# Reordering the start of a fused Fourier-filter and SiLU-MLP kernel: t2 loads between the filters and the weights, six stage-1 result tiles, four inverse tiles, weight roundings behind the groups, three vector pieces moved

## The chip, the cores and the metric

One core of one Trainium2 chip. The metric is the device time of one execution in microseconds (us); every time below is a median of several executions. Profiles are of one execution each, so a profile's span can differ from the median by a few us. In the lines of the profile PE is TensorE (matmuls), PEld its weight loads, DVE VectorE, ACT ScalarE and POOL GpSimd; SPq and ACTq are the queues on which the sync engine and ScalarE issue DMAs. L198 is line 198 of the kernel of that run, "x4" four instructions merged into one line, and a bracket tells how long the engine was idle before and what ended it.

## The reference, cut to what matters

```python
# x: (8, 3008, 256) float32; filters: (1505, 256); weights float64
X = np.fft.rfft(x, axis=1)
y = np.fft.irfft(X * (filt_r + 1j * filt_i)[None], n=3008, axis=1)     # global filter
h = y.reshape(8 * 3008, 256) @ w_in                                     # 256 -> 2048
g = h * (1 / (1 + np.exp(-h)))                                          # silu
return g @ w_out                                                        # 2048 -> 256
```

## The kernel before

The kernel does the Fourier part as matmuls in four stages per batch: sums and stage 1 (results `t1`, stored to DRAM as `d1`), six groups of forward transform, filter product and inverse transform (load `t2`, multiply, add, inverse, result tiles `q`, stored as `d2`), and stage 3 (load `t4`, results `y`). The MLP runs in 384 "hidden steps" and fills TensorE. Batches 1 to 7 do their Fourier part beside the steps of the batch before; batch 0 has nothing to hide behind. Its Fourier part and the conversion of the float64 weights ("roundings", 16 of them, on DVE, ACT and GpSimd) are the ramp. The parts concerned:

```python
def load_filters():                       # 16 DMAs, each to 16 partitions, 12 rows of 1 KB
    for j in range(4):
        for half in range(2):
            for k, filt in enumerate((filt_r, filt_i)):
                nc.sync.dma_start(out=f_t[k][p0:p0 + 16]..., in_=...)
...
def stage1(u):
    t1 = tpool.tile(..., tag="t")         # two buffers, shared with t2
    ...                                   # four matmuls, two copies out of PSUM
    nc.gpsimd.dma_start(out=d1..., in_=t1...)     # twice
...
weights(0); load_filters()                # the ramp's order
# sums and stage1, u = 0..7
load_t2(0); load_t2(1); e_t; weights(1); weights(2); wi_t
rounded(0); rounded(1)
for g in range(6):
    forward(g)                            # its end loads t2 of g + 2
    multiply(g, 0); multiply(g, 1)        # DVE
    add(g, 0); add(g, 1)                  # GpSimd in batch 0
    if g > 0: inverse(g - 1)              # its copies, then four stores issued by ACT
    if g % 2 == 0: weights(3 + g // 2)
    rounded(2 + g)
inverse(5); load_t4(0); rounded(8); rounded(9)
# stage3(0..3); then the steps, with rounded(10..15) in steps 0 to 5
```

```python
def plan(b, part):                        # batches 1 to 7; at = first step of batch b
    put(at - 49, 0, load_x, 0); put(at - 49, 0, load_x, 1)
    for u in range(8):
        put(at + u - 48, 5, sums, u); put(at + u - 47, 3, stage1, u)
    ...
    for g in range(NG):                   # every third step from at - 37
        put(at + 3 * g - 37, 3, forward, g) ...
```

## Time and profile before

| | before |
|---|---|
| median (4 executions) | 2746.07 us (2745.39 to 2747.09) |
| TensorE busy | 2630.5 of 2745.5 us |
| first t2 load issued | 63.66 us |
| multiplies of groups 0 to 5 start | 71.0, 80.3, 89.1, 98.4, 107.1, 116.3 |
| t4 load issued | 130.84 |
| first matmul of step 0 | 146.43 |
| step 7 starts | 206.3 |

How to read it: TensorE is busy for 96% of the span, so I looked for time to win where it idles: nearly all before 200 us, the rest in small holes. The start of a step is read off one instruction which each step has once (ACT's first copy of `px`); the difference of such starts between two kernels shows in which step time was won. For step 0 this line reads, before and in the changed kernel:

```profile
147.66 0.37 ACT L447 COPY abc<-px 128x256 f32<-128x256 f32 x1 [1.33 <-PE px L439]
```
```profile
127.86 0.37 ACT L459 COPY abc<-px 128x256 f32<-128x256 f32 x1 [1.33 <-PE px L451]
```

### The profile page before, as it was taken

What the parts mean: (1) busy time and instruction counts of PE and PEld (TensorE: products, weight loads), DVE (VectorE), ACT (ScalarE), POOL (GpSimd) and SP (SyncE); (2) the same over time, 40 slices, a digit from 0 to 9 for tenths busy, and PEclk for the clock granted to TensorE, in tenths of its full rate; (3) what the DMA queues carried; (4) which work ended last, traced back from release to release, by engine and by line L of the source; (5) the groups of instructions that cost most, each with busy time, mean ns of one, the idle gap of its engine ahead of it and who ended that gap; (6) DMA issues with size and microseconds to landing.
All of it is one profiled execution on the core that took longest, in us unless ns stands there. A gap on an engine that the chain in (4) does not pass through costs nothing.

```text
span 2745.5 us, 45764 instructions
## 1 busy us (share of the span) xinstructions
PE 2630.5 (96%) x17664; PEld 2198.8 (80%) x17664; DVE 1652.4 (60%) x3492; ACT 1098.9 (40%) x2994; POOL 506.0 (18%) x738
## 2 busy tenths in 40 slices
PE   2489999999999999999999999999999999999998
PEld 0368889788887888878887888878888788898987
DVE  3676655666556665666656665566655666555555
ACT  1244344433444334443444434444344433444443
POOL 2541210211111111112111121022111211110100
PEclk9789999999999999999999999999999999999999
DMA  9643221331214221332113312133121421110000
GB/s 176 192 125 79 49 46 32 88 79 40 46 37 105 65 50 23 71 85 68 35 33 82 81 47 44 35 82 85 39 47 31 107 65 43 32 27 20 9 16 15
DMA packets 187929, 166.94 MB, mean 61 GB/s; under 512 B 122176, under 2 KB 155584, under 8 KB 187456
## 3 DMA queue, kind: packets, MB, share of 16 engines
q1 hardware_dynamic: 165912, 111.89, 18.0%
q0 software_dynamic: 16256, 47.20, 6.8%
q10 hardware_dynamic: 5544, 4.93, 0.8%
q8 instruction: 138, 2.26, 0.3%
q14 instruction: 79, 0.65, 0.1%
HBM read 88.96 MB, written 74.97 MB: 60 GB/s over the span
## 4 chain that ended last, share of the span: by engine, by line
PE 90%; DVE 4%; DMA 2%; ACT 1%; issue 1%; ACTq 0%; SPq 0%; POOL 0%; DVEq 0%; POOLq 0%
PE acc L495 40%; PE px L439 24%; PE pyz L439 17%; PE pc L330 3%; PE pd L358 3%; PE pa L277 2%; PE pb L300 2%; DMA d<-t 1%; DVE g L410 1%; DVE u L265 1%; DMA x<-in_x_dram 1%; ACTq L338 0%; DVE z L321 0%; DMA raw<-in_moe_w_out_dram 0%; DVE z L320 0%
## 5 line engine op out<-in xcount | busy, mean ns | idle before, releaser
L495 PE MATMUL acc<-g,w_t 128*128 128x256 f32 (+1 forms) x5376 | 1512.5, 375 | 0.4 <-DVE g L410 0.4
L495 PEld LDWEIGHTS acc<-g,w_t 128*128 128x128 f32 x5376 | 1021.9, 190 | 115.6 <-DVE g L410 0.8
L410 DVE TENSOR_TENSOR g<-pyz,abc 128x256 f32<-128x256 f32 (+1 forms) x1152 | 478.2, 415 | 569.3 <-ACT abc L460 323.0
L410 DVE TENSOR_TENSOR g<-g 128x256 f32<-128x256 f32 (+3 forms) x1152 | 611.8, 531 | 196.6 <-ACT g L443 183.4
L439 PE MATMUL px<-ty,w_t 128*128 128x256 f32 (+1 forms) x2304 | 695.4, 383 | 3.5 <-ACT abc L454 2.9
L443 ACT ACTIVATE g<-g 128x256 f32<-128x256 f32 (+1 forms) x1152 | 472.8, 410 | 244.8 <-DVE g L410 244.8
L439 PEld LDWEIGHTS px<-ty,w_t 128*128 128x128 f32 x2304 | 420.5, 190 | 128.5 <-issue 71.0
L439 PE MATMUL pyz<-y,w_t 128*128 128x256 f32 (+1 forms) x1536 | 456.3, 379 | 10.9 <-DVE g L410 10.9
L410 POOL TENSOR_TENSOR s<-s 128x256 f32<-128x256 f32 (+1 forms) x329 | 266.4, 827 | 1022.2 <-DVE s L513 999.0
L439 PEld LDWEIGHTS pyz<-y,w_t 128*128 128x128 f32 x1536 | 282.0, 189 | 58.8 <-DVE g L410 20.1
L454 ACT COPY abc<-px 128x256 f32<-128x256 f32 (+1 forms) x384 | 141.2, 368 | 373.3 <-PE px L439 373.3
L443 ACT ACTIVATE g<-px 128x256 f32<-128x256 f32 (+1 forms) x384 | 145.8, 380 | 302.1 <-PE px L439 302.1
L460 ACT COPY abc<-px 128x256 f32<-128x256 f32 (+1 forms) x384 | 142.9, 372 | 285.2 <-PE px L439 284.9
L338 POOL DMA_DIRECT2D d<-q x168 | 99.3, 598 | 713.5 <-DVE q L208 705.6
L439 PE MATMUL px<-y,w_t 128*128 128x256 f32 (+1 forms) x768 | 226.2, 376 | 1.0 <-ACT y L210 1.0
L439 PE MATMUL pyz<-ty,w_t 128*128 128x256 f32 (+1 forms) x768 | 226.7, 377 | 0.0
L439 PEld LDWEIGHTS pyz<-ty,w_t 128*128 128x128 f32 x768 | 145.2, 190 | 19.0 <-DVE g L410 2.9
L439 PEld LDWEIGHTS px<-y,w_t 128*128 128x128 f32 x768 | 144.3, 190 | 19.6 <-ACT y L210 1.1
L447 ACT COPY abc<-px 128x256 f32<-128x256 f32 (+1 forms) x384 | 134.1, 349 | 1.3 <-PE px L439 1.3
L282 POOL DMA_DIRECT2D d<-t x128 | 65.6, 516 | 332.1 <-ACT abc L460 283.7
L330 PE MATMUL pc<-z,e_t 64*128 64x256 f32 x768 | 106.0, 413 | 16.0 <-POOL z L320 13.4
L208 DVE COPY y<-pd 128x376 f32<-128x376 f32 x64 | 51.7, 808 | 100.7 <-PE pd L358 100.7
(49 smaller groups left out, 1306.9 us busy)
## 6 DMA issues: line engine op xcount, KB each, us to landing
d<-t POOLq DMA_DIRECT2D x128, 192.0 KB, 3.0
t<-d SPq DMA_DIRECT2D x96, 256.0 KB, 3.9
t<-d SPq DMA_DIRECT2D x128, 192.0 KB, 3.9
d<-q POOLq DMA_DIRECT2D x168, 128.0 KB, 2.6
out_dram<-o SPq DMA_DIRECT2D x636, 32.0 KB, 1.8
x<-in_x_dram SPq DMA_DIRECT2D x120, 128.0 KB, 3.0
x<-in_x_dram SPq DMA_DIRECT2D x120, 60.0 KB, 2.9
raw<-in_moe_w_in_dram SPq DMA_DIRECT2D x16, 256.0 KB, 4.8
```

The lines of the kernel that those rows point to most:

```text
L277: nc.tensor.matmul(out=ps[h][64 * par:64 * par + 64], lhsT=wf_t[rows, par], rhs=ut[rows, par], start=True, stop=True)
L282: nc.gpsimd.dma_start(out=d1[par].rearrange("s p n c -> (s p) n c")[:, 4 * u:4 * u + 4, :], in_=t1[64 * par:64 * par + 2 * NS].rearrange(" ...
L330: nc.tensor.matmul(out=ps[i][:, k, :], lhsT=e_t[rows, g, k, ri, :], rhs=zs[k][rows, ri, :], start=(ri == 0), stop=(ri == 1))
L338: queue.dma_start(out=d2[a0:a0 + 2, :, :].rearrange("s n c -> n s c"), in_=qt[64 * p:64 * p + 64, :, :])
L358: nc.tensor.matmul(out=ps[h][c0:c0 + 64, cb, i, :], lhsT=t4s[g][rows, i, 128 * cb + c0:128 * cb + c0 + 64], rhs=wi_t[rows, :], start=True, ...
L410: eng.tensor_tensor(out=out, in0=in0, in1=in1, op=op)
L439: nc.tensor.matmul(out=out, lhsT=w_t[:, c, 0, jp], rhs=rhs, start=start, stop=True, skip_group_check=True)
L443: nc.scalar.activation(out=g[:, k, 0:n], in_=g[:, k, 0:n] if src is None else src, func=AFT.Silu)
L447: nc.scalar.copy(out=sums[:, 0, 0:n], in_=xo)
L454: nc.scalar.copy(out=sums[:, 1, 0:n], in_=xo)
L460: nc.scalar.copy(out=sums[:, 2, 0:n], in_=xo)
L495: nc.tensor.matmul(out=acc[pair][i][:, h, 0:n], lhsT=w_t[:, c, 1, jp], rhs=g[:, k, 0:n], start=(jp == 0 and h == 0), stop=last, skip_group ...
```

## The change

Intent: give stage 1 so many result tiles that hardly a copy waits for a store, let the first t2 loads pass two thirds of the filters and all later weights, take the weight roundings out of the groups' path, and move three vector pieces of the steady part away from busy places. The core of the diff:

```diff
-    def load_filters():
+    def load_filters(first, last):
...
+            if b > 0 or u < 2 or u > 5:
+                t1 = tpool.tile(..., tag="t")
+            elif u < 4:
+                t1 = typool.tile(..., tag="ty")
+            else:
+                t1 = us["t1"][:, u - 4]          # a tile of the g pool
...
-            eng = nc.vector if b > 0 else nc.gpsimd
+            eng = nc.vector if b > 0 or (g == NG - 1 and k == 0) else nc.gpsimd
...
+                if b > 0 or i == 0:
+                    qt = qpool.tile(..., tag="q")
+                else:
+                    qt = opool.tile(..., tag="o")
...
-                    queue = nc.gpsimd if b > 0 else nc.scalar
+                    queue = nc.gpsimd if b > 0 or (g == NG - 1 and i == 0) else nc.scalar
...
-        put(at - 49, 0, part["load_x"], 0)                 # and 1
+        put(at - 51, 0, part["load_x"], 0)
-            put(at + u - 48, 5, part["sums"], u)
+            put(at + u - (48 if u else 49), 5, part["sums"], u)
-        for g in range(NG):                                # steps 3 g - 37
+        for g, step in enumerate((-37, -34, -31, -28, -25, -21)):
+            late = 4 if g == 4 else 0                      # group 4's adds half a step later
...
-    load_filters()
+    load_filters(0, 4)
...
-    weights(1)
-    weights(2)
         part["forward"](g)
+        if g == 0:
+            load_filters(4, 2 * NG)
+        if g < 3:
+            weights(1 + g)
         ...                                                # multiplies, adds
+        if 2 <= g < NG - 1:
+            rounded(g)
         if g > 0:
             part["inverse"](g - 1)
-        rounded(2 + g)
     part["inverse"](NG - 1)
+    weights(4)
     part["load_t4"](0)
-    rounded(8)
-    rounded(9)
+    for j in range(5, 9):
+        rounded(j)                                         # weights(5) after j = 5
...                                                        # rounded(9..15) in steps 0 to 5, two of them in step 5
-    stores: ((28, 5), (29, 1))
+    stores: ((30, 1), (30, 5))
```

More of the change, by code (lines that the diff above doesn't have):

```diff
@@ L198, in load_filters @@
                     nc.sync.dma_start(
-                        out=f_t[k][p0:p0 + 16].rearrange("p g k c -> p (g k) c"),
-                        in_=bass.AP(tensor=filt.tensor, offset=filt.offset + off * C,
-                                    ap=[[94 * C, 16], [t * C, 2 * NG], [1, C]]))
+                        out=f_t[k][p0:p0 + 16].rearrange("p g k c -> p (g k) c")[:, first:last],
+                        in_=bass.AP(tensor=filt.tensor, offset=filt.offset + (off + t * first) * C,
+                                    ap=[[94 * C, 16], [t * C, last - first], [1, C]]))
     flip = [0]
@@ L236, in load_x @@
                 queue = (nc.sync, nc.scalar)[u % 2]
+                if u == 0:
+                    us["t1"] = gpool.tile([128, 2, 2, 2, C], FP32, name="t1_g", tag="g")
                 if u in (0, 2):
@@ L271, in stage1 @@
             ut = us.pop(u)
-            t1 = tpool.tile([128, 2, 2, C], FP32, name=f"t1_{b}_{u}", tag="t")
+            if b > 0 or u < 2 or u > 5:
+                t1 = tpool.tile([128, 2, 2, C], FP32, name=f"t1_{b}_{u}", tag="t")
+            elif u < 4:
+                t1 = typool.tile([128, 2, 2, C], FP32, name=f"t1_{b}_{u}", tag="ty")
+            else:
+                t1 = us["t1"][:, u - 4]
             ps = [bank(b, f"pa_{b}_{u}_{h}") for h in range(2)]
@@ L332, in inverse @@
             for i in range(2):
-                qt = qpool.tile([128, 2, C], FP32, name=f"q_{b}_{g}_{i}", tag="q")
+                if b > 0 or i == 0:
+                    qt = qpool.tile([128, 2, C], FP32, name=f"q_{b}_{g}_{i}", tag="q")
+                else:
+                    qt = opool.tile([128, 2, C], FP32, name=f"q_{b}_{g}_{i}", tag="o")
                 evac(qt, ps[i])
@@ L379, in plan @@
         at = STEPS * b
-        put(at - 49, 0, part["load_x"], 0)
-        put(at - 49, 0, part["load_x"], 1)
+        put(at - 51, 0, part["load_x"], 0)
+        put(at - 51, 0, part["load_x"], 1)
         for u in range(8):
-            put(at + u - 48, 5, part["sums"], u)
+            put(at + u - (48 if u else 49), 5, part["sums"], u)
             put(at + u - 47, 3, part["stage1"], u)
@@ L386, in plan @@
         put(at - 39, 0, part["load_t2"], 1)
-        for g in range(NG):
-            put(at + 3 * g - 37, 3, part["forward"], g)
-            put(at + 3 * g - 37, 5, part["multiply"], g, 0)
-            put(at + 3 * g - 36, 1, part["multiply"], g, 1)
-            put(at + 3 * g - 36, 5, part["add"], g, 0)
-            put(at + 3 * g - 35, 1, part["add"], g, 1)
-            put(at + 3 * g - 35, 3, part["inverse"], g)
+        for g, step in enumerate((-37, -34, -31, -28, -25, -21)):
+            late = 4 if g == 4 else 0
+            put(at + step, 3, part["forward"], g)
+            put(at + step, 5, part["multiply"], g, 0)
+            put(at + step + 1, 1, part["multiply"], g, 1)
+            put(at + step + 1, 5 + late, part["add"], g, 0)
+            put(at + step + 2, 1 + late, part["add"], g, 1)
+            put(at + step + (3 if late else 2), 3, part["inverse"], g)
         put(at - 18, 5, part["load_t4"], 0)
@@ L641 @@
     nc.sync.dma_start(out=e_t, in_=e_dram.ap())
-    weights(1)
-    weights(2)
-    nc.sync.dma_start(out=wi_t, in_=wi_dram.ap())
     rounded(0)
@@ L648 @@
         part["forward"](g)
+        if g == 0:
+            load_filters(4, 2 * NG)
+            nc.sync.dma_start(out=wi_t, in_=wi_dram.ap())
+        if g < 3:
+            weights(1 + g)
         for k in range(2):
@@ L652 @@
             part["add"](g, k)
+        if 2 <= g < NG - 1:
+            rounded(g)
         if g > 0:
             part["inverse"](g - 1)
-        if g % 2 == 0:
-            weights(3 + g // 2)
-        rounded(2 + g)
     part["inverse"](NG - 1)
+    weights(4)
     part["load_t4"](0)
-    rounded(8)
-    rounded(9)
+    for j in range(5, 9):
+        rounded(j)
+        if j == 5:
+            weights(5)
     for g in range(4):
@@ L667 @@
         plan(b, spectral(b))
-    for k in range(6):
-        put(k, 1, rounded, 10 + k)
-        if k in (1, 3):
-            put(k, 1, weights, 6 + k // 2)
+    for j in range(9, NJ):
+        put(*((j - 9, 1) if j < NJ - 1 else (5, 5)), rounded, j)
+        if j in (11, 13):
+            put(j - 9, 1, weights, j // 2 + 1)
     per = len(PAIRS) * 2
-    stores = (((10, 1), (10, 5)), ((19, 5), (20, 1)), ((28, 5), (29, 1)), ((34, 1), (34, 5)),
+    stores = (((10, 1), (10, 5)), ((19, 5), (20, 1)), ((30, 1), (30, 5)), ((34, 1), (34, 5)),
               ((42, 1), (42, 5)), ((50, 1), (51, 1)))
```

## The prediction

> **What bounds the kernel now.** I read the slices of the page first, then busy time by stretch, then the waits of the first 260 us, the sync engine's queue in that stretch, and last the few places where TensorE still idles later. The page, 40 slices of 68.6 us, and its span line:
>
> ```profile
> span 2745.5 us, 45764 instructions
> PE   2489999999999999999999999999999999999998
> PEclk9789999999999999999999999999999999999999
> ```
>
> TensorE is full from the fourth slice to the end: 2630.5 of 2745.5 us busy. Idle is 115 us in all, so a change that adds and removes no matmul (this one doesn't) can win at most 115/2746 = 4.2%, and only in the ramp (three slices) or in small holes later. By stretch (columns: stretch, length, busy us of PE, weight load, DVE, ACT, POOL, then granted clock, DMA share, GB/s):
>
> ```profile
> 60.00:80.00 20.00, 8.88 (x80) 4.59 (x80) 9.86 (x18) 3.70 (x6) 9.91 (x15) 1.00 0.89 282
> 80.00:100.00 20.00, 10.98 (x128) 6.66 (x128) 14.52 (x24) 3.66 (x6) 13.86 (x19) 0.91 0.95 254
> 191.00:200.00 9.00, 7.95 (x40) 5.68 (x39) 8.09 (x15) 4.03 (x10) 4.56 (x6) 1.00 0.22 70
> 206.80:213.00 6.20, 6.20 (x33) 4.51 (x32) 3.94 (x9) 2.32 (x6) 1.00 (x2) 1.00 0.15 34
> ```
>
> The ramp is bound by DMA and by chains, not by one engine. From 146 to 200 us the first six hidden steps run with DVE about 90% busy (8.09 of 9.00): step starts, read off the first ACT copy of each, are 147.7, 155.6, 164.6, 173.2, 181.8, 190.5 and 199.1, so 8.6 us a step against 7.26 once the roundings are over. The ramp's waits (engine, line waited for, us, times, longest), and the sync engine's issues (start, length):
>
> ```profile
> ACT t L210 <- DMA d<-t: 38.2, 6, 16.4
> DVE t L208 <- DMA d<-t: 34.7, 5, 14.5
> PE pb L300 <- DMA t<-d: 28.7, 6, 20.0
> ```
> ```profile
> 20.64 0.51 SPq L198 DMA_DIRECT2D filt<-in_filt_r_dram  x1
> 44.34 0.32 SPq L198 DMA_DIRECT2D filt<-in_filt_i_dram  x1
> 63.66 2.71 SPq L289 DMA_DIRECT2D t<-d  x4
> 130.84 13.76 SPq L344 DMA_DIRECT2D t<-d  x10
> ```
>
> Stage 1 has data by 17.5 us, but its result tiles (two buffers) wait for their stores, and the stores share the DMA engines with 3.1 MB of filters until 58 us. So the first t2 load starts at 63.66. Then six groups run at 9.0 us each (first multiplies at 80.3, 89.1, 98.4, 107.1, 116.3); the load of t4 is issued at 130.84 and step 0 begins at 146.4.
>
> The steady holes: all windows from 300 to 2527 us together show 9.35 us without TensorE, about 1.5 us a batch, in two places. One, on DVE at the batch boundary (start, length):
>
> ```profile
> 486.36 0.65 DVE L513 COPY s<-acc 128x480 f32<-128x480 f32 x1
> 486.93 1.78 DVE L265 TENSOR_TENSOR u<-x 111x512 f32<-111x512 f32 x2
> 488.63 0.40 DVE L515 COPY s<-acc 128x240 f32<-128x240 f32 x1
> 488.95 0.41 DVE L410 TENSOR_TENSOR g<-pyz,abc 128x256 f32<-128x256 f32 x1
> ```
>
> The sums of the next batch stand between two drain copies and hold back the g that TensorE's next matmul waits for (0.97 us). The other is at 332 to 335 us: the adds of group 4 (0.42 and 0.92) stand between the same copies, 0.57 us.
>
> **What the Trainium skill says.** (1) "SBUF — State Buffer", section "Door 1: The DMA port swizzle": partitions 0 to 15 reach 4 of 16 ports, measured there at 104 GB/s. A filter DMA writes 16 partitions; the trace agrees: 192 KB every 1.85 us is 106 GB/s, while weights and tables to 128 partitions moved at 370 to 400. (2) "DMA: Bandwidth & Descriptors", "Queues, rings and completion order": each DMA engine consumes the descriptors of one ring in order. The trace agrees: the t2 load of group 2, issued at 77.45 behind two pairs of weights, let its matmul start only at 84.32. (3) "SBUF — State Buffer", "SBUF: two separate sides": VectorE and GpSimd share a port pair which one instruction holds to its end. The trace agrees: a rounding's DVE piece of 0.42 takes 0.94 beside a GpSimd piece. (4) "TensorE: Matmul & The Clock Gate", "What's actually happening": idle windows halve the clock; here 0.59 to 0.70 was granted at 100 to 160 us. The changed ramp has gaps too, so I credit nothing for the clock.
>
> **The change, part by part.**
>
> Stage 1 (six result tiles, a third of the filters ahead of the t2 loads). Results 0 to 5 no longer wait for a buffer; 6 and 7 wait for the stores of 0 and 1, which land at 25 to 26 us as before. All evacuations are done by about 27 us, all stores issued by 28 (eight pairs at 1 us of POOL). Bytes from 17.5 us on: d table and first weights 1.84 MB at some 400 GB/s, 4.6 us; filters 1.05 MB (was 3.15) at 106, 9.9 us; t1 stores 3.1 MB at 250 to 300 GB/s (they ended alone at about that rate at 62 us), 11 us. Sum 25.5 us if nothing overlaps: 43 us. Check on before: from 26.9 to 57.9, 2.75 MB of filters (26 us) plus 1.5 MB of stores (5.5) make 31.5; it took 31.0. So the t2 load starts at about 43 instead of 63.7: -20.7. Roundings 0 and 1 fit in 36 to 42.
>
> Groups. Group 0 shifts with it: forward at 46.5, multiplies 50 to 52.5; group 1 follows at 52.6 to 55, for the rounding between them is gone. Then the remaining filters come in the sync queue after t2 of group 2: 2.1 MB at 106 GB/s is 20 us, starting at about 54, with 0.5 MB of d2 stores beside (2 us): the multiplies of group 2 start at 76 (were at 89.1). So the roundings taken out of the groups gain little there; the filters take their place. Behind them, in order, come weights 1, t2 of group 3, weights 2, t2 of 4, weights 3, t2 of 5. With one group's d2 stores each is 2.1 MB at 275 GB/s (mean of 75 to 100 us), 7.6 us: t2 lands at 82, 89.5 and 97. DVE needs 2.4 (multiplies) + 3.2 (rounding) + 0.6 (copy) = 6.2 a group, POOL 2.8 + 1.4 + sometimes 2.9 = 7.1, both below 7.6. Group 5: multiplies 97.5 to 100, its adds halved by the move of one to DVE, inverse matmuls to 107, copies and stores landed at 111 (before: 14.5 us from multiply to t4, now about 13.5). The load of t4 starts 20 us earlier.
>
> Stage 3. Before it took 15.6 us from t4's issue to step 0. Now four roundings (5 to 8) at 3.3 us, 13 us of DVE, lie between the last inverse and the evacuations: from 107 to 120, while stage 3 can have its matmuls from 115 on; and 1 MB of weights stands before the second t4 load. I add 2.5 us: step 0 at 111 + 18 = 129, -17.5.
>
> Steps 0 to 5. Before, six roundings lie in them; now seven, the last two both in step 5, where DVE is full: +2.7. The batch-1 sums leave step 0 (1.5 us of DVE) but stand before its first combine and wait for x, whose loads are issued only after the last t4 load (144.6 before; 3.3 us to landing): +0.8. Sum +3.5.
>
> Steady state. Sums one step earlier: 6 x 0.97 = 5.8. Group 4's adds later: 7 x 0.57 = 4.0. I take 8.5 of these 9.8; the new places (step 47, steps 25 to 30) have DVE below 65%.
>
> Sum: -17.5 + 3.5 - 8.5 = -22.5; 2745.9 - 22.5 = 2723.
>
> **Rivals.** (a) The filters don't hold the groups: they move beside other traffic, group 2 starts at about 65, and groups run at DVE's and POOL's 6 to 7 us.[...] Against: DMA share was 0.9 to 1.0 while filters ran at 104 to 140 GB/s. Then t4 would load at some 98, the four roundings would bind stage 3, and the time would be about 2712. (b) The stores of t1 don't gain: their tiles are free, but the same engines serve them, and a queue with more stores outstanding is no faster; the t2 load would start at about 52, filters and all behind it by 9 later: 2732. (c) DVE takes the gain back: roundings before stage 3 and in step 5, each 4.3 instead of 3.3 because POOL's products stand beside them, and the moved adds meet other pieces: 2730 to 2735.
>
> **Range and chances.** The ramp sum is uncertain by about 8 either way, the steady part by 3. I predict 2723, with 2710 to 2736. A gain over 2% would need a time under 2691, that is 55 of the 115 us; a loss over 2% would need a broken order of buffers.
>
> **What would show it.** The t2 load at 43 (40 to 47); multiplies of group 2 waiting for the filters' DMA, starting near 76; t4 loading near 111; step 0 near 129 and step 5 over 11 us long; no wait of TensorE over 0.3 us for g at the batch boundary. It is wrong if group 2 starts before 68 or the t2 load after 50, or if the steady windows still lack 1.5 us a batch.

## The result, and the profile after

The changed kernel takes 2717.35 us (2717.07 to 2718.15, 4 executions) against 2746.07: ratio 0.9896, interval 0.9878 to 0.9913. Ratios are the mean time of one kernel's runs over that of the other's of the same rounds, so they are not quite the ratio of the medians quoted. It is 28.7 us faster, 1%, and lies inside the predicted range (2710 to 2736), 5.6 below the predicted 2723.

The page's span and slices of the changed kernel:

```profile
span 2716.4 us, 45798 instructions
PE   4589999999999999999999999999999999999998
PEclk9699999999999999999999999999999999999999
```

The first slice is fuller than before (4 against 2). TensorE's busy sum is 2626.7 us, so it still idles for 89.7 us (before 115.0). The sync engine's issues (start, length):

```profile
38.83 2.75 SPq L296 DMA_DIRECT2D t<-d  x4
47.02 0.60 SPq L198 DMA_DIRECT2D filt<-in_filt_r_dram  x1
63.74 0.32 SPq L198 DMA_DIRECT2D filt<-in_filt_i_dram  x1
108.57 0.80 SPq L354 DMA_DIRECT2D t<-d  x2
```

The first t2 load goes out at 38.8 (was 63.7). The second part of the filters takes the queue from 47.0 to 63.7 and the t4 load comes at 108.6 (was 130.8). What the filters do to the groups stands on DVE, in order of time (last column: idle before, and what ended it):

```profile
54.28 0.69 DVE L208 COPY q<-pc 128x512 f32<-128x512 f32 x1
71.55 0.69 DVE L319 TENSOR_TENSOR z<-pb,filt 128x512 f32<-128x512 f32 x1 [16.58 <-DMA filt<-in_filt_r_dram]
80.67 0.69 DVE L319 TENSOR_TENSOR z<-pb,filt 128x512 f32<-128x512 f32 x1 [1.96 <-PE pb L307]
```

Group 2's multiplies wait 16.6 us for the filters and start at 71.6, 17.5 us earlier than before, though group 0's started 25.3 earlier (45.7). The late part by stretch, columns as in the prediction:

```profile
300.00:2500.00 2200.00, 2199.64 (x14852) 1859.25 (x14851) 1340.89 (x2875) 913.96 (x2515) 373.31 (x553) 1.00 0.24 56
```

0.36 us of 2200 without TensorE: the two holes of each batch are gone. At the batch boundary DVE now reads

```profile
463.53 1.28 DVE L267 TENSOR_TENSOR u<-x 111x512 f32<-111x512 f32 x2
469.44 0.65 DVE L525 COPY s<-acc 128x480 f32<-128x480 f32 x1
470.27 0.41 DVE L527 COPY s<-acc 128x240 f32<-128x240 f32 x1 [0.17 <-PE acc L507]
470.70 0.42 DVE L422 TENSOR_TENSOR g<-pyz,abc 128x256 f32<-128x256 f32 x1
```

with the sums 6 us ahead of the drain copies instead of between them. The account by step starts of both profiles (differences of the starts, us):

| stretch | before | changed | difference |
|---|---|---|---|
| to the start of step 0 | 147.66 | 127.86 | -19.80 |
| step 0 | 7.92 | 8.41 | +0.49 |
| steps 1 to 4 | 34.87 | 34.48 | -0.39 |
| step 5 | 8.62 | 11.41 | +2.79 |
| step 6 | 7.27 | 8.44 | +1.17 |
| step 7 to the end | 2539.16 | 2525.80 | -13.36 |
| span | 2745.5 | 2716.4 | -29.1 |

### The profile page after: what moved, and what is told of

Read it like the earlier page. It is cut to its first block, busy times and chain, and to the rows that moved or that the text cites. A ratio compares the mean times of both kernels' runs of the same rounds, so it can differ in the third digit from the quotient of the medians. Undisturbed runs are those within 1.5% of the kernel's fastest.

```text
span 2716.4 us, 45798 instructions
## 1 busy us (share of the span) xinstructions
PE 2626.7 (97%) x17664; PEld 2203.4 (81%) x17664; DVE 1654.5 (61%) x3494; ACT 1099.1 (40%) x2994; POOL 505.1 (19%) x738
## 4 chain that ended last, share of the span: by engine, by line
PE 93%; DMA 3%; DVE 2%; issue 1%; ACT 1%; SPq 0%; POOL 0%; ACTq 0%; DVEq 0%
PE acc L507 41%; PE px L451 25%; PE pyz L451 18%; PE pc L337 3%; PE pd L368 2%; PE pa L284 2%; PE pb L307 2%; DMA x<-in_x_dram 1%; DVE g L422 0%; DMA filt<-in_filt_i_dram 0%; DMA raw<-in_moe_w_out_dram 0%; DVE u L267 0%; DMA e_t<-e_tbl 0%; DMA d<-q 0%; DMA t<-d 0%
## 5 line engine op out<-in xcount | busy, mean ns | idle before, releaser
L451 PEld LDWEIGHTS px<-y,w_t 128*128 128x128 f32 x768 | 144.6, 190 | 22.5 <-issue 3.0
```

The source lines that it names most:

```text
L451: nc.tensor.matmul(out=out, lhsT=w_t[:, c, 0, jp], rhs=rhs, start=start, stop=True, skip_group_check=True)
```

## The experiments

All runs gave a correct result but one. Because chips and calls differ by about 1 us, each is compared with the kernel before of the same call; "against the changed kernel" compares these differences (the changed kernel: -28.7). Medians of four executions each. Executions of one kernel spread over 1 to 7 us, so differences under about 3 us between two versions are not settled by time alone, and I say where the profile decides.

### e_steady: the steady moves alone

```diff
  (the kernel before, with only plan() and the third store pair of the change)
```

> The kernel before with only the moves in the plan of batches 1 to 7 (x loads two steps and the first sums one step earlier, group 4's adds half a step later, group 5 one step later, the third store pair moved). Theory (the moves themselves close the two holes per batch): 13 us less than before, about 2733, and no wait of TensorE for g over 0.3 us after step 7. Rival (the holes went because the new ramp shifts the batches against their transfers): no gain, about 2746.

2739.48 against 2745.77, ratio 0.9978 (0.9964 to 0.9993): only 6.3 less. From step 7 to the end the profile has 2526.55, 12.6 less than before, as the theory says. But step 0 took 12.10 us instead of 7.92, and DVE shows why:

```profile
146.34 0.89 DVE L412 TENSOR_TENSOR ty<-y,ty 128x256 f32<-128x256 f32 x2
150.83 1.29 DVE L265 TENSOR_TENSOR u<-x 111x512 f32<-111x512 f32 x2 [3.60 <-DMA x<-in_x_dram]
152.04 0.42 DVE L412 TENSOR_TENSOR g<-pyz,abc 128x256 f32<-128x256 f32 x1
```

The moved sums of batch 1 stand ahead of step 0's first combine and wait 3.6 us for x, whose loads are issued only behind the last t4 load. In the changed kernel the same sums start at 128.15 without a wait, because there DVE is late itself (four roundings until 122, then stage 3's copies and the tokens until 128.1) and x, whose loads are issued from 122.3 on, lands meanwhile. So the two parts of the change aren't independent: alone, the steady moves lose 4.2 us of what they win. (What is then left of the gap to 13 is within the spread between executions: the profiled span was 9.6 less.)

### e_ramp: the ramp alone

```diff
  (the changed kernel, with plan() and the store steps of the kernel before)
```

> The changed kernel with the plan of batches 1 to 7 and the store steps put back as before; the new ramp stays. Theory (ramp and steady part add up): the 13 us come back, about 2731, with the holes of 0.97 and 0.4 us in TensorE again. Rival (the steady gain comes from the ramp): stays at about 2717.

2731.46 against 2745.77, ratio 0.9947 (0.9932 to 0.9962). 14.3 less than before, 14.4 more than the changed kernel: the theory's number. Step 7 to the end is back at 2539.42, and TensorE waits for g again (12 times, 8.4 us from 300 us on, as in the kernel before). The steady gain comes from the moves, not from the ramp.

### e_two_t1: two stage-1 tiles again

```diff
-            if b > 0 or u < 2 or u > 5:
-                ... (six tiles)
+            t1 = tpool.tile([128, 2, 2, C], FP32, name=f"t1_{b}_{u}", tag="t")
```

> The changed kernel with the stage 1 results in two tiles again; filters stay split. Theory (the tiles let all stores be issued by 32 us): evacuations wait for stores again, the first t2 load is issued near 50 instead of 38.8, and the time is about 10 us longer, 2727. Rival (only the filters' bytes mattered, the tiles gain nothing): t2 load at 39 to 41, time 2717 to 2719.

2724.80 against 2745.77, ratio 0.9923 (0.9907 to 0.9940): 7.8 us of the gain lost. The copies do wait for stores again:

```profile
ACT t L210 <- DMA d<-t: 17.8, 6, 7.5
DVE t L208 <- DMA d<-t: 14.3, 4, 8.0
```

(waits from 15 to 50 us, columns as in the prediction; before they were 38.2 and 34.7.) The t2 load comes at 42.72, 3.9 later than with six tiles, not 11 later as expected; step 0 starts 5.8 later (the rest of the 7.8 is not placed). So the tiles count, but with a third of the filters ahead two tiles are only a little worse in stage 1.

### e_filters_all: all filters ahead of the t2 loads

```diff
-    load_filters(0, 4)
+    load_filters(0, 2 * NG)
...
-            load_filters(4, 2 * NG)
```

> The changed kernel with all filters loaded ahead of the t2 loads, as before; six tiles stay. Theory (the filters cost some 30 us of the DMA engines wherever they stand): the first t2 load is issued at 54 to 58, but group 2 no longer waits for filters and its multiplies start at 70 to 76 against 71.6, so the time is 2717 to 2724. Rival (the split hides the filters behind other work): everything is some 17 us later, about 2734.

2715.61 against 2745.77, ratio 0.9891 (0.9877 to 0.9906): 1.4 less than the changed kernel, not settled by time. The profile says what happens: t2 load at 48.23 (9.4 later), multiplies of group 0 at 63.1 (17.4 later), of group 2 at 73.7 (2.1 later), of group 5 at 94.5 (2.1 earlier), t4 at 106.5. The theory holds, though the t2 load came before the 54 to 58 that it named: for the groups from 2 on, the filters cost about the same wherever they stand, and the split wins nothing when the rest of the change is there. With all filters ahead in both, the t2 load still comes 15.4 us earlier than in the kernel before (63.66): there the last eight stage-1 stores were issued only from 44.6 to 61.3, because the two tiles came free late; in this run all sixteen are issued by 30.4.

### v_queues and v_all_queues: filters from two queues

```diff
-            for half in range(2):
+            for half, queue in halves:                     # upper 16 partitions of each block on ACT's queue
-                    nc.sync.dma_start(
+                    queue.dma_start(
```

> The changed kernel with the second part of the filters issued from two queues: the lower 16 partitions of each block by the sync engine, the upper 16 by ACT. Theory (a 16-partition write is held to a quarter of the ports, and two queues fill two quarters at once): the multiplies of group 2 start at about 62 instead of 71.6 and the time falls by 6 to 9, to about 2709. Rival (the 16 engines are simply full, or descriptors in line on one engine set the pace): group 2 at 69 to 72, time 2716 to 2718.

2717.35 against 2744.98, ratio 0.9899 (0.9884 to 0.9913): no gain. Group 2's multiplies start at 70.2. ACT's half went out between 32.9 and 43.7, but the other transfers paid: group 0 started 3.7 us later (49.4), and the first inverse waited until 58.3 for its table (50.8 in the changed kernel).

> All filters ahead of the t2 loads (as in e_filters_all), lower halves by the sync engine, upper halves by ACT after its stage 1 copies. Theory (ports): the first t2 load at 40 to 43 instead of 48.2, the multiplies of group 0 at 50 to 53 instead of 63.1, groups at 7 us from there, step 0 some 8 us earlier than in e_filters_all: about 2707. Rival (engines full): t2 load at 48, multiplies at 63, 2714 to 2717.

2718.04 against 2744.98, ratio 0.9898 (0.9882 to 0.9915): t2 load at 43.6 instead of 48.2, near the theory, but group 0 at 61.6 and group 5 at 96.4; no gain. The times of both runs went the rival's way: with a second queue the groups come no earlier. v_queues also moved half of the filters' second part ahead of the t2 loads, so it isn't a pure test of the queue. The runs don't tell whether descriptors in line or full engines are the reason.

### x_filt128: the filters' cost by itself

```diff
-        for j in range(4): ... for half in range(2): ...   # eight DMAs to 16 partitions for each filter
+        for k, filt in enumerate((filt_r, filt_i)):        # one DMA to 128 partitions, same bytes, 1 KB rows
+            nc.sync.dma_start(out=f_t[k]...[:, first:last], in_=(rows 11 apart, counted downwards))
```

> The disputed cost by itself; wrong filters on purpose. The changed kernel with each filter part loaded by one DMA to 128 partitions, the same 1 KB rows and the same bytes, instead of eight DMAs to 16 partitions. Theory (the narrow destination holds the filters to a quarter of the ports, about 100 GB/s): both parts move at some 350 GB/s, the multiplies of group 2 start at 56 to 60 instead of 71.6, the groups follow 7 to 8 us apart, time about 2707. Rival (1 KB rows or the engines themselves set the pace, which the run with two queues speaks for): group 2 at 69 to 72, time 2715 to 2718. The result is wrong in both.

2706.64 against 2745.98, ratio 0.9863 (0.9846 to 0.9879): 10.6 less than the changed kernel, the time that the theory named. The result is wrong (relative error 1.4). The stretch from 47 to 72 us, first in the changed kernel, then in this run (last three columns: granted clock, DMA share, GB/s):

```profile
47.00:72.00 25.00, 7.71 (x86) 5.18 (x71) 4.90 (x8) 0.58 (x1) 5.55 (x8) 0.77 0.95 162
```
```profile
47.00:72.00 25.00, 14.35 (x114) 7.90 (x114) 14.28 (x23) 3.88 (x6) 10.96 (x15) 0.73 0.95 273
```

The engines are equally "busy" (0.95), but move 273 instead of 162 GB/s; group 2 starts at 54.4 instead of 71.6. The groups behind it lay 11.8, 9.2 and 7.2 apart, not 7 to 8, so of 17.1 us at group 2 there are 13.6 left at the t4 load (94.97) and 10.6 in the time. A row size of 1 KB is not what makes the filters slow. The run changes two things with the width, the number of DMAs (4 for 32) and the rows read, so it doesn't prove the ports; it shows that the 32 narrow DMAs with their rows cost 10.6 us. It also bears on stage 1: with the first part wide, the t2 load comes at 36.69, only 2.1 us earlier than 38.83.

### e_round_after: the roundings behind the inverse, within the groups

```diff
-        if 2 <= g < NG - 1:
-            rounded(g)
         if g > 0:
             part["inverse"](g - 1)
+        if 2 <= g < NG - 1:
+            rounded(g)
```

> The changed kernel with the rounding of groups 2 to 4 emitted after the inverse of the group before, as in the kernel before. Theory (there DVE waited 2.3 us a rounding for ACT, which first waited for the inverse's copy and issued four stores): groups 3 to 5 start 9 us apart instead of 7.4 to 9.1, DVE shows waits of over 2 us for ACT's first rounding piece, time 2720 to 2722. Rival (transfers of t2 set the distance of the groups): starts as now, time 2717 to 2718.

2723.59 against 2744.98, ratio 0.9920 (0.9905 to 0.9935): 7.3 more than the changed kernel, somewhat over the 3 to 5 expected. Groups 3 to 5 start at 81.5, 91.7 and 100.9 instead of 80.7, 88.1 and 96.7. From 70 to 115 us:

```profile
DVE work L595 <- ACT work L591: 10.4, 4, 3.1
```

DVE waits 10.4 us for ACT's rounding piece in four roundings, because in ACT's program the inverse's copy and four stores stand before it. The changed kernel has one such wait left, 3.9 us for rounding 5 behind the last inverse. Where a rounding stands relative to the inverse was worth 7.3 us here; how many roundings stand in the groups was not tested by itself.

### e_pieces: small pieces of the ramp undone

```diff
-  eng = nc.vector if b > 0 or (g == NG - 1 and k == 0) else nc.gpsimd
+  eng = nc.vector if b > 0 else nc.gpsimd
-  (four inverse tiles, one store pair of group 5 on GpSimd's queue)
+  (two inverse tiles, all of batch 0's stores on ACT's queue)
```

> The changed kernel with the ramp's small pieces undone: four inverse tiles back to two, the first adds of group 5 back on GpSimd, its stores back on ACT's queue. Theory (they shorten the tail from group 5 to t4 only): the t4 load is issued 2 to 3 us later than 108.6, time 2718 to 2720. Rival 1 (copies wait for the tiles' stores in each group): 5 us or more. Rival 2 (no part of the path): 2717.

2719.66 against 2744.98, ratio 0.9908 (0.9893 to 0.9922): 3.4 more than the changed kernel, which is near the theory in time. In its profile, though, the place that the theory named does not show it: t4's load came at 108.61, the same moment, with group 5 starting 1.0 us earlier: 13.0 us from group 5's multiplies to t4 instead of 11.9. One us is shown (the profiled spans are 2717.5 and 2716.4); the rest of the 3.4 is not placed.

### v_early, v_x, v_stores: versions meant to be better

```diff
(v_early, on the changed kernel)
+            weights(1)                       # ahead of the filters' second part
             load_filters(4, 2 * NG)
...
+        if g == 1: rounded(2); rounded(3)    # into DVE's wait for the filters
+        (rounded(4), rounded(5) in groups 3 and 4; weights(5) ahead of load_t4(0); rounded(6..9) behind the groups)
+    for j in range(10, NJ): put(j - 10, 1, rounded, j)     # one a step
(v_x: besides, weights(4), weights(5) and the first two x loads of batch 1 issued in group 5)
(v_stores: besides, group 4's four stores issued by the sync engine)
```

> A version meant to beat both. Weights 1 go ahead of the filters' second part, roundings 2 and 3 into DVE's idle stretch before group 2, roundings 4 and 5 into groups 3 and 4, 6 to 9 behind the groups, 10 to 15 one to a step; weights 5 ahead of the t4 loads. Theory (two roundings in step 5 cost 4 us there, DVE is idle from 55 to 71): step 5 takes 8.6 instead of 11.4, step 6 7.3 instead of 8.4, group 2 starts 3 us later, which the later t2 loads hide; 2712 to 2714. Rival (the later filters push every group back): 2716 to 2719.

2714.10 against 2745.98, ratio 0.9888 (0.9873 to 0.9903): 3.2 less than the changed kernel. Step 5 takes 8.64 and step 6 7.27, as expected, and group 2 started 2.1 later. But step 0 took 11.00: the sums again waited for x (1.9 us), since DVE was free earlier.

> v_early with weights 4 and 5 and the first two x loads of batch 1 issued in group 5, ahead of its stores. Theory (in v_early and in e_steady step 0 took 11 and 12.1 us because the moved sums stand before its first combine and wait for x loads issued only after the last t4 load): step 0 takes 7 to 8.5, the rest as in v_early, about 2711. Rival (step 0 is long for another reason, or the x bytes push the stores of group 5 back as much): 2714.

2712.67 (2708.86 to 2714.08) against 2745.45, ratio 0.9880 (0.9863 to 0.9896). Step 0 is down to 8.50, the sums wait for nothing. It has the lowest median of the correct versions, 4.1 less than the changed kernel by differences. The intervals of the two overlap, so "better" rests on the step times of the profiles more than on the clock.

> v_x with the four stores of group 4's inverse issued by the sync engine, which is free then, instead of ACT. Theory (ACT issues six stores between 96.7 and 102.6 and so copies the last inverse tile late): the t4 load is issued 2 us earlier than in v_x, time 1 to 2 us less, about 2709.5. Rival (the stage behind, with four roundings on DVE, sets the end): as v_x.

2714.71 against 2745.45, ratio 0.9886 (0.9870 to 0.9903): no gain; the expectation fell. The sync engine was not free:

```profile
96.82 7.54 SPq L252 DMA_DIRECT2D x<-in_x_dram  x8
104.46 4.79 SPq L350 DMA_DIRECT2D d<-q  x4
111.19 1.72 SPq L356 DMA_DIRECT2D t<-d  x4
```

It was held in issuing the x loads until 104.46, so the stores and the t4 load came later than in v_x (107.08).

## Why the prediction was right, and where it was not

**The sum and its parts.** Predicted -17.5 (start of step 0), +3.5 (steps 0 to 6), -8.5 (steady): -22.5. The profiles have -19.8, +4.06, -13.36: -29.1. Each part has the right sign; the steady part was mis-sized most. The prediction's ceiling of 115 us, the idle time of TensorE, is not quite one: its idle time fell by 25.3 us and the span by 29.1, for the same matmuls were also counted busy for 3.8 us less.

**Stage 1.** Predicted t2 load at 43, measured 38.8. The failing step is "Sum 25.5 us if nothing overlaps": stores and filters do overlap. It took 21.3 us from 17.5, not 25.5. From 17 to 39 us the core moved 6.35 MB, 289 GB/s, where the sum had 9.9 us for the filters alone; in x_filt128 the same bytes in wide DMAs brought the t2 load only 2.1 us forward. The check on the kernel before that seemed to confirm the sum (31.5 against 31.0) doesn't carry over: there stores were held by the two tiles too (no store was issued between 29.2 and 44.6), not only by bandwidth, so its agreement may be luck. (The prediction's pace of a filter DMA every 1.85 us is a little slow: the issues from 28.30 to 44.34 lie 1.78 apart, 110 GB/s.)

**Groups.** Predicted that the second part of the filters would hold group 2 until 76; it held it until 71.6. The mechanism is the predicted one: the filters were issued from 47.0 instead of 54 and took 24.5 us instead of 22. Rival (a) had group 2 start at 65 and t4 load at 98; the 16.6 us wait at group 2 and the t4 load at 108.6 speak against it, and e_filters_all shows the same total with the filters in front. Other traffic did go on beside them, though: 4 MB moved from 47 to 72 us, of which 2.1 were filters. Predicted "7.6" us between t2 loads; the groups' starts lay 9.1, 7.4 and 8.6 apart, and group 5 came at 96.7 (predicted 97.5). The right total partly hides a cause I had not put in: e_round_after shows 7.3 us hanging on the order of rounding and inverse, which I had counted only as "3.2 (rounding)" of DVE.

**Stage 3.** Predicted 18 us from t4 to step 0; from 108.57 to the first matmul of step 0 at 126.64 are 18.07. That DVE's roundings would hold up stage 3 was right:

```profile
107.25 0.69 DVE L595 SCALAR_TENSOR_TENSOR work<-raw,work 128x512 f32<-128x512 uint32 x1 [3.92 <-ACT work L591]
122.15 2.07 DVE L208 COPY y<-pd 128x376 f32<-128x376 f32 x3
```

The equal total is partly luck. The four roundings took DVE from 102.57 to 122.15, 19.6 us instead of 13: the first waited 3.9 us for ACT, and the other three took 4.4 each instead of 3.3, as rival (c) had said. They also began 4.4 us earlier than the predicted 107, and from their end to step 0 there were 4.5 us instead of 9.

**Steps 0 to 5.** Two roundings in step 5: predicted +2.7, measured +2.79, and another 1.17 in step 6, which I had left out. The wait for x in step 0 (+0.8) did not show, since the roundings hid it; step 0 grew by 0.49. e_steady shows the wait unhidden: 3.6 us on DVE.

**Steady state.** The two holes closed as predicted, and e_ramp shows that the moves of the plan did it (as a whole: no run separates group 4's adds from group 5 and the store pair, which moved in the same steps). The failing step is "6 x 0.97 = 5.8 ... 7 x 0.57 = 4.0", of which I even took less. Its second half was also misread. In the profile before, TensorE waits 0.43 to 0.44 us for g at group 4, in six of seven batches; the third and fourth lines below are the batch that has no wait, where the second add took 0.42 instead of 0.92 us:

```profile
333.45 0.92 DVE L321 TENSOR_TENSOR z<-z,p 128x256 f32<-128x256 f32 x1
335.07 0.70 PE L439 MATMUL pyz<-y,w_t 128*128 128x256 f32 x2 [0.44 <-DVE g L410]
660.30 0.42 DVE L321 TENSOR_TENSOR z<-z,p 128x256 f32<-128x256 f32 x1
661.42 0.70 PE L439 MATMUL pyz<-y,w_t 128*128 128x256 f32 x2
489.41 0.70 PE L439 MATMUL pyz<-y,w_t 128*128 128x256 f32 x2 [0.97 <-DVE g L410]
```

(The last line is the hole at the batch boundary.) The step starts show 1.23 to 1.25 us won at each of six batch boundaries, 7.4 in all, and 6.0 in all at and behind group 4 (at it about 1.1 in six batches and 0.4 in the one without a wait): 13.4. I had sized a hole by the idle time of matmuls, 0.97; the step lost more. My reading, which no run tests, is that the matmuls around the hole also run less tightly (from 300 us on, the `pyz` weight loads waited 17.2 us for g in the kernel before and 6.0 in the changed one, the `pyz` matmuls 8.4 and none). Perfetto Trace Analysis of the Trainium skill, section "Identifying the Most-Contended Engine", calls matmul busy time no good measure of how close a kernel is to its limit, because pipelined instructions "look smaller in the trace". It says that of a whole kernel, not of one stall; here it was the idle time that looked too small, 0.97 against 1.24.

**Rivals (b) and (c).** Rival (b) said a queue with more stores outstanding is no faster and the t2 load would come at 52; it came at 38.8, and taking the tiles away again cost 7.8 us (e_two_t1). Rival (c) was right in kind (step 5, step 6) and, before stage 3, in the length of a rounding (4.4 us against its 4.3), but the gain was not lost.

**What stays open.** Why two queues don't speed up narrow filters; what of x_filt128's gain is width and what is the number of DMAs or the rows; some 2 us of e_pieces. The parts of the ramp undone one at a time give 7.8 (tiles), 7.3 (order of rounding and inverse), 3.4 (small pieces) and -1.4 (split), 17.1 in sum against 14.3 for the ramp alone: they overlap, or the difference is spread between runs. No run tests by itself the new place of the weight loads behind the t2 loads, or of the roundings taken out of the groups.

## What to carry to other kernels

Size a stall by the shift of a repeated instruction between two profiles, not by the idle time at the stall. A transfer that is slow in itself was not hidden here by cutting it in two and moving one part to another busy place; more buffers, so that other transfers needn't wait behind it, and a rounding placed before the inverse instead of behind it are what won here. And a piece of vector work moved to "earlier" takes its own inputs' loads with it: check which loads now end on the path.

## What the Trainium skill lacked or had wrong

- SBUF — State Buffer: it has no rate for a narrow write beside other transfers, and I found none on another page. Stores from 48 partitions and filters to 16, together with loads to 128, moved 289 GB/s from 17 to 39 us; from 47 to 72 us, with the filters' second part, the core moved 162 GB/s, and 273 when the filters went to 128 partitions.
- DMA: Bandwidth & Descriptors: I found no figure for how long an issuing engine is held when much is outstanding. Issuing eight x loads took the sync engine 7.5 us (in another run 9.3), and it stood from 48.1 to 53.1 us between two filter DMAs. The profile's waits name earlier transfers that had not landed (for the second case 5.0 us, a t2 load); what makes the engine wait for them, no run shows.
- Perfetto Trace Analysis: nothing on how to size a single stall; the number here is 0.97 us of idle against 1.24 us lost.
